# Attention of batches 2 to 7 with its large transposes on VectorE instead of TensorE

## The chip, the cores and the metric

One core of a Trainium2 chip runs the kernel. It has a TensorE (PE in the rows; PEld is its weight load), a VectorE (DVE), a ScalarE (ACT), a GpSimd (POOL) and a SyncE (SP), which issues most of the DMAs. The metric is device time in microseconds of one execution, as the median of several runs. About 0.2% of it (2.2 us) is what a measurement of this kernel can tell from no change.

## The reference

```python
# x: 8 batches x 8 heads x 512 tokens x 64;  state: 8 x 8 x 32 slots x 64
scores  = x @ state.T / 8;   a  = softmax(scores)  over the 32 slots;    xread = a  @ state
scores2 = state @ x.T / 8;   a2 = softmax(scores2) over the 512 tokens;  sread = a2 @ x
y = concat(xread, sread)     # per batch 512 + 32 rows; 4352 rows in all, 8 heads x 64 = 512 columns
h = relu(y @ w1_in) ** 2;    y = h @ w1_out          # 512 -> 2048 -> 512
h = y @ w2_in;  h = layernorm(h * softmax(h)) * g;   out = h @ w2_out    # 512 -> 1024 -> 512
```

Everything is float32. The kernel keeps that precision by splitting each operand into a high and a low float32r part and multiplying three times (high by high, high by low, low by high).

## The kernel before, in words

**The first MoE.** Its rows are worked off in nine blocks: eight batches of 512 token rows and, last, the slot rows of all batches. A block goes through 16 steps, one for each 128 of the 2048 hidden columns. In a step `hidden` multiplies the attention weights `ah`, `al` (two tiles, 128 partitions x 2 x 512) by `sw`, which is state times w1_in for that batch, so that xread is never formed: six matmuls of 512 columns into `ps_h`. ScalarE and VectorE form `r` (relu, then its square), `high` casts it to `gh`, `low` subtracts to `gl`, and `project` multiplies `gh`, `gl` by w1_out into four accumulators `acc`: 12 matmuls. A step's `project` follows the `hidden` of the step two later, so that the chain r, gh, gl has time. A step is thus 18 matmuls, and everything else on TensorE is put between them.

**sw.** The product state times w1_in lies in DRAM (`sw_d`). For four steps at a time, `load_sw` fetches it to a staging tile `stg` in DMAs on SP, and `split_sw` makes the two `sw` tiles from it: a copy on ScalarE (L119) and a subtraction on VectorE (L120). `hidden` waits for both.

**Attention of one batch** is spread over the steps of the batch before it. x of the batch comes by four DMAs in `xs`, tokens on partitions (L441). `trans_x` turns a pair of heads by four 128x128 TensorE transposes into a PSUM bank `ps_x` (L135), and `split` makes `xh`, `xl`. `scores_t` multiplies by the state, laid out block diagonally (two matmuls, L482 and L483); ScalarE copies one half of the result (L487) and VectorE adds the other (L488), so that a tile `st` holds the scores of four heads x 32 slots on partitions and 512 tokens on columns. From it two softmaxes are made.
- Over slots: `rows_a` transposes `st` to tokens on partitions (by_token, `ps_r`, L494), reduces, subtracts and takes Exp (`e`); `rows_b` sums and scales; `trans_a` transposes `e` back (`ps_a`, L135) and splits it into `ah`, `al`.
- Over tokens: `cols_a` and `cols_b` work on `st` in place (Exp with an accumulated sum, L529, then a scaling, L536); `cols_t` transposes to tokens on partitions (`ps_c`), and `sread` multiplies by x in `xs`.

**What sets the order.** Batches 0 and 1 are written out by hand. From batch 2 on, the source gives the work step by step, and a scheduler orders each engine's instructions by its own estimates when the kernel is built; on the chip each engine then runs its list in that order and waits where an operand isn't ready. `xs` has one buffer, so x of the next batch is loaded after `sread` of this one.

Of the kernel before, what the change touches and what calls it, by code (L numbers as in the profile page):

```python
# [8 lines left out]
F32 = mybir.dt.float32  # L9
F32R = mybir.dt.float32r  # L10
# [10 lines left out]
def memory_attention_relu2_solu(  # L21
# [15 lines left out]
    nc = tc.nc  # L37
    P = 128
    B, H, S, D = x.shape
# [4 lines left out]
    SO = S + NS  # L44
    NT = S // P
    NHP = H // 2
# [44 lines left out]
    xsp = pool("xsp", 1, sa, side="right")  # L91
    xtp = pool("xtp", 1, sa, side="right")
    atp = pool("atp", 2, sa, side="right")
# [3 lines left out]
    ps_a = pool("ps_a", 1, sb, space=PSUM)  # L97
# [20 lines left out]
    def split(hi, lo, src):  # L118
        nc.scalar.activation(out=hi, in_=src, func=AF.Copy)  # L119
        nc.vector.tensor_tensor(out=lo, in0=src, in1=hi.bitcast(F32), op=ALU.subtract)  # L120

    def split_bank(hi, lo, ps):

        nc.scalar.activation(out=hi, in_=ps, func=AF.Copy)

        def rest():
            nc.tensor.matmul(out=ps, lhsT=negi, rhs=hi, start=False, stop=True, skip_group_check=True)
            nc.scalar.activation(out=lo, in_=ps, func=AF.Copy)

        return rest  # L130
# [17 lines left out]
    def bank(name):  # L148
        return ps_m.tile([P, 512], F32, tag="m", name=name)
# [284 lines left out]
    xs_t = {}  # L434
    a1_t = {}

    def load_x(b):
        pl, tag = (wp, "w") if b == 1 else (xsp, "xs")
        xs_t[b] = pl.tile([P, NT, H, D], F32, tag=tag, name="xs")
        for t in range(NT):  # L440
            nc.sync.dma_start(out=xs_t[b][:, t], in_=x[b].rearrange("h (p t) d -> t p h d", t=NT)[t])  # L441

    def attention(b):

        v = {}

        def new_a1():
            a1_t[b] = tuple(a1p.tile([P, NQ, S], F32R, tag=t, name=t) for t in ("ah", "al"))

        def trans_x(hp):  # L450
            ps = ps_a.tile([P, 512], F32, tag=f"acc{hp}", name="ps_x") if b < 2 else bank("ps_x")
            transposes(ps, [xs_t[b][:, t, 2 * hp : 2 * hp + 2].rearrange("p h d -> p (h d)") for t in range(NT)])
            if b == 0:
                xh = gp.tile([P, S], F32R, tag="gh", name="xh")
                xl = gp.tile([P, S], F32R, tag="gl", name="xl")
            elif b == 1:

                if hp == 0:
                    new_a1()
                xh, xl = (a1_t[b][k][:, hp % 2, :] for k in range(2))  # L460
            else:
                xh = xtp.tile([P, S], F32R, tag="xh", name="xh")
                xl = xtp.tile([P, S], F32R, tag="xl", name="xl")
            v["rest", "x", hp] = (split_bank if b < 2 else split)(xh, xl, ps)
            v["xt", hp] = (xh, xl)

        def scores_t(hp):
# [22 lines left out]
        def by_token(tp, ps):  # L490
            for t in range(2):
                for q in range(NQ):
                    o = (t * NQ + q) * P
                    nc.tensor.transpose(  # L494
                        ps[:, o : o + P], v["st", q][:, (2 * tp + t) * P : (2 * tp + t + 1) * P], ident
                    )

        def rows_a(tp):

            ps = bank("ps_r")  # L500
            by_token(tp, ps)
            mx = smp.tile([P, 2 * H], F32, tag="mx", name="mx")
            s3 = ps.rearrange("p (g n) -> p g n", n=NS)
            nc.vector.tensor_reduce(out=mx, in_=s3, axis=AX.X, op=ALU.max)
            e = atp.tile([P, 512], F32, tag="e", name="e1")
            e3 = e.rearrange("p (g n) -> p g n", n=NS)
            nc.vector.tensor_tensor(
                out=e3, in0=s3, in1=mx.unsqueeze(2).to_broadcast([P, 2 * H, NS]), op=ALU.subtract
            )
            nc.scalar.activation(out=e, in_=e, func=AF.Exp, scale=scale)  # L510
            v["e1", tp] = e
# [55 lines left out]
        def trans_a(q):  # L567
            if q == 0 and b != 1:
                new_a1()
            ps = bank("ps_a1")  # L570
            e = [v["e1", tp].rearrange("p (t k) -> p t k", t=2) for tp in range(NT // 2)]
            transposes(ps, [e[t // 2][:, t % 2, q * P : (q + 1) * P] for t in range(NT)])
            v["rest", "a", q] = (split_bank if b < 2 else split)(a1_t[b][0][:, q, :], a1_t[b][1][:, q, :], ps)

        def rest(*k):
            v.pop(("rest", *k))()
# [29 lines left out]
    acc = {}  # L606
# [163 lines left out]
    def trans(ln):  # L770
# [7 lines left out]
            split(lh[:, a * 512 : (a + 1) * 512], ll[:, a * 512 : (a + 1) * 512], ps)  # L778
        return lh, ll

    def down(blk, t, lh, ll, final):

        ps = pools["o"].tile([P, DM], F32, tag="o", name="ps_o")
        for k in range(NK):
            wt = w2[NM + k // 2]
            o = (k % 2) * 512
            a, bb = lh[:, k * P : (k + 1) * P], ll[:, k * P : (k + 1) * P]
            nc.tensor.matmul(out=ps, lhsT=a, rhs=wt[:, 0, o : o + 512], start=(k == 0), stop=False)  # L788
            nc.tensor.matmul(out=ps, lhsT=a, rhs=wt[:, 1, o : o + 512], start=False, stop=False)  # L789
            nc.tensor.matmul(out=ps, lhsT=bb, rhs=wt[:, 0, o : o + 512], start=False, stop=(k == NK - 1))  # L790
            yield k + 1
        ob = gp.tile([P, DM], F32, tag="gh", name="ob")
        if final:

            to = out[blk * SO : blk * SO + S].rearrange("(p t) e -> p t e", t=NT)[:, t, :]
            nc.scalar.activation(out=ob[:, : DM // 2], in_=ps[:, : DM // 2], func=AF.Copy)
            nc.vector.tensor_copy(out=ob[:, DM // 2 :], in_=ps[:, DM // 2 :])
            nc.scalar.dma_start(out=to[:, : DM // 2], in_=ob[:, : DM // 2])
            nc.sync.dma_start(out=to[:, DM // 2 :], in_=ob[:, DM // 2 :])
            return  # L800
        nc.scalar.activation(out=ob, in_=ps, func=AF.Copy)
        if blk < B:
            nc.sync.dma_start(out=out[blk * SO : blk * SO + S].rearrange("(p t) e -> p t e", t=NT)[:, t, :], in_=ob)
        else:
            per = P // NS
            for bb in range(per):
                b = t * per + bb
                nc.sync.dma_start(out=out[b * SO + S : (b + 1) * SO], in_=ob[bb * NS : (bb + 1) * NS, :])
# [26 lines left out]


    att = [attention(0), attention(1)]
    steps = {}
    hid, sq, ready, left = {}, {}, {}, {}
# [66 lines left out]
    for s, (b, f) in enumerate(items):  # L906
        if s < 4 * FPC:
            continue
        w, ws = divmod(s, NF)
# [35 lines left out]
        h = high(*squares.pop(0)) if squares else None  # L945
# [4 lines left out]
        if att:  # L950
            for part in att.pop(0):
                part()
        if ws == 0 and 1 <= w < B - 1:
            load_x(w + 1)
        n = S if b < B else NSR
        if h:
# [11 lines left out]
        for e in ends.get(b, ())[1:]:  # L968
            i = f - e + 3
# [31 lines left out]
    order = [blk for blk, t in tiles if t == 0]  # L1001
# [13 lines left out]
    for s in range(1, len(tiles) + 2):  # L1015
        if s == 1:
            reload_w2(7, 1)
        if s < len(tiles):
            blk, t = tiles[s]
            i = order.index(blk) + 1  # L1020
# [7 lines left out]
            ps = up(s, blk, t)  # L1028
# [42 lines left out]
```

## Time and profile before

| | us |
|---|---|
| median of 3 runs (lowest, highest) | 1117.78 (1117.42, 1118.1) |
| span of the profiled execution | 1115.4 |
| TensorE busy | 1096.8 (98%) |
| VectorE busy | 708.5 (64%) |
| ScalarE busy | 512.4 (46%) |

The profiled execution's span is 1115.4 us; the median device time stands 2.4 us above it, which is what lies outside the span. TensorE is busy for nearly all of it; the others are averages over stages that differ much.

### The profile page before, as it was taken

The numbers are of one execution on the slowest core, as the hardware profiler recorded it, in microseconds if no ns is written. First come the engines' busy times: TensorE is split into PE (matmuls) and PEld (weight loads), VectorE is DVE, ScalarE is ACT, GpSimd is POOL, SyncE is SP. The second block draws the span as 40 slices with busy tenths as digits, with TensorE's granted clock in tenths as the row PEclk, the third lists the DMA queues.
The fourth block names the chain that finished last, engine by engine and source line by source line (L and its number), as shares of the span: only waits on it lengthen the run. The fifth ranks groups of instructions, "written<-read, shape, count | busy, mean of one in ns | idle before, by whom it ended". The sixth has DMA issues, their size and how long they took to land.

```text
span 1115.4 us, 15150 instructions
## 1 busy us (share of the span) xinstructions
PE 1096.8 (98%) x5692; PEld 911.2 (82%) x5692; DVE 708.5 (64%) x1358; ACT 512.4 (46%) x903; POOL 44.7 (4%) x62
## 2 busy tenths in 40 slices
PE   5899999999999999999999999999999999999998
PEld 4788888888888888888888889888888888888887
DVE  7999995687686695884755446664545545455443
ACT  6899776455454452442333113343433334234232
POOL 1000000010000000000000000000000000000000
PEclk9899999999999999999999999999999999999999
DMA  9779883767766632412112027410101101000001
GB/s 275 253 229 311 273 276 85 239 199 221 215 198 181 200 130 69 149 62 79 40 38 76 25 91 263 151 57 20 67 19 58 67 20 41 26 20 29 20 19 38
DMA packets 93017, 134.69 MB, mean 121 GB/s; under 512 B 44816, under 2 KB 45584, under 8 KB 92944
## 3 DMA queue, kind: packets, MB, share of 16 engines
q1 hardware_dynamic: 92224, 133.46, 37.2%
q8 instruction: 45, 0.74, 0.3%
q10 hardware_dynamic: 720, 0.26, 0.1%
q14 instruction: 28, 0.23, 0.1%
HBM read 83.37 MB, written 49.28 MB: 119 GB/s over the span
## 4 chain that ended last, share of the span: by engine, by line
PE 93%; DVE 4%; ACT 1%; DMA 1%; issue 0%; ACTq 0%; POOL 0%; DVEq 0%; POOLq 0%
PE h L738 16%; PE acc L144 11%; PE acc L145 11%; PE acc L146 11%; PE ps_h L144 6%; PE ps_h L145 6%; PE ps_h L146 6%; PE ps_o L790 6%; PE ps_o L789 6%; PE ps_o L788 6%; PE ps_t L777 3%; PE ps_sr L553 2%; PE ps_x L135 1%; PE ps_sw L388 1%; PE ps_sw L389 1%; PE ps_c L494 1%
## 5 line engine op out<-in xcount | busy, mean ns | idle before, releaser
L144 PE MATMUL acc<-gh,w1out 128*128 128x512 f32 (+1 forms) x576 | 219.0, 380 | 0.0
L146 PE MATMUL acc<-gh,w1out 128*128 128x512 f32 (+1 forms) x576 | 217.9, 378 | 0.0
L145 PE MATMUL acc<-gl,w1out 128*128 128x512 f32 (+1 forms) x576 | 217.8, 378 | 0.0
L738 PE MATMUL h<-w,x2h 128*128 128x512 f32 x544 | 148.6, 395 | 0.0
L618 ACT ACTIVATE r<-ps_h 128x512 f32<-128x512 f32 (+1 forms) x144 | 82.4, 572 | 141.1 <-PE ps_h L146 139.6
L620 DVE TENSOR_TENSOR r<-r,ps_h 128x512 f32<-128x512 f32 (+1 forms) x112 | 72.4, 647 | 89.7 <-ACT r L618 89.1
L146 PEld LDWEIGHTS acc<-gh,w1out 128*128 128x128 f32 x576 | 108.4, 188 | 20.6
L144 PEld LDWEIGHTS acc<-gh,w1out 128*128 128x128 f32 x576 | 108.4, 188 | 20.4 <-DVE ev_x L657 0.2
L145 PEld LDWEIGHTS acc<-gl,w1out 128*128 128x128 f32 x576 | 108.4, 188 | 19.9
L738 PEld LDWEIGHTS h<-w,x2h 128*128 128x128 f32 x544 | 99.6, 188 | 18.9
L144 PE MATMUL ps_h<-ah,sw 128*128 128x512 f32 x256 | 107.1, 418 | 0.0
L788 PE MATMUL ps_o<-w,lh 128*128 128x512 f32 x272 | 106.0, 390 | 0.0
L790 PE MATMUL ps_o<-w,ll 128*128 128x512 f32 x272 | 105.9, 390 | 0.0
L789 PE MATMUL ps_o<-w,lh 128*128 128x512 f32 x272 | 105.8, 389 | 0.0
L634 DVE TENSOR_TENSOR gl<-r,gh 128x512 fp32r<-128x512 f32 (+1 forms) x144 | 96.4, 669 | 11.7 <-ACT r L627 8.7
L756 ACT ACTIVATE e<-h,nm 128x1024 f32<-128x1024 f32 x34 | 38.0, 1117 | 138.8 <-DVE nm L753 138.8
L146 PE MATMUL ps_h<-ah,sw 128*128 128x512 f32 x256 | 100.9, 394 | 0.0
L145 PE MATMUL ps_h<-al,sw 128*128 128x512 f32 x256 | 100.6, 393 | 0.0
L752 DVE TENSOR_REDUCE nm<-h 128x1 f32<-128x1024 f32 x34 | 41.6, 1224 | 82.6 <-PE h L738 82.6
L738 PE MATMUL h<-w,x2l 128*128 128x512 f32 x272 | 83.8, 389 | 0.0
L764 ACT ACTIVATE j<-e,mu 128x1024 f32<-128x1024 f32 x34 | 39.1, 1151 | 54.3 <-DVE mu L761 50.3
L738 PEld LDWEIGHTS h<-w,x2l 128*128 128x128 f32 x272 | 51.1, 188 | 10.8
(173 smaller groups left out, 1723.4 us busy)
## 6 DMA issues: line engine op xcount, KB each, us to landing
stg<-sw_d SPq DMA_DIRECT2D x120, 128.0 KB, 3.1
sw_d<-ev_sw SPq DMA_DIRECT2D x28, 512.0 KB, 4.0
st<-in_moe_w_out_dram SPq DMA_DIRECT2D x24, 512.0 KB, 4.8
xs<-in_x_dram SPq DMA_DIRECT2D x32, 256.0 KB, 4.2
w1i_d<-w1in SPq DMA_DIRECT2D x16, 512.0 KB, 4.7
st<-in_moe_w_in_dram SPq DMA_DIRECT2D x16, 512.0 KB, 5.3
w1in<-w1i_d SPq DMA_DIRECT2D x32, 256.0 KB, 4.6
x_d<-ev_x SPq DMA_DIRECT2D x16, 512.0 KB, 2.7
```

The costliest lines, as they stand in the source:

```text
L144: nc.tensor.matmul(out=ps, lhsT=lh, rhs=rh, start=first and i == 0, stop=False)
L145: nc.tensor.matmul(out=ps, lhsT=lh, rhs=rl, start=False, stop=False)
L146: nc.tensor.matmul(out=ps, lhsT=ll, rhs=rh, start=False, stop=last and i == n - 1)
L618: nc.scalar.activation(out=r, in_=ps, func=AF.Relu)
L620: nc.vector.tensor_tensor(out=r, in0=r, in1=ps, op=ALU.mult)
L634: nc.vector.tensor_tensor(out=gl, in0=r, in1=gh.bitcast(F32), op=ALU.subtract)
L738: nc.tensor.matmul(out=ps[:, a * 512 : (a + 1) * 512], lhsT=lt[:, k, t * P : (t + 1) * P], rhs=w2[k][:, i, a * 512 : (a + 1) * 512], start ...
L752: nc.vector.tensor_reduce(out=nm, in_=ps, axis=AX.X, op=ALU.max)
L764: nc.scalar.activation(out=j, in_=e, func=AF.Square, bias=mu, accum_out=var)
L788: nc.tensor.matmul(out=ps, lhsT=a, rhs=wt[:, 0, o : o + 512], start=(k == 0), stop=False)
L789: nc.tensor.matmul(out=ps, lhsT=a, rhs=wt[:, 1, o : o + 512], start=False, stop=False)
L790: nc.tensor.matmul(out=ps, lhsT=bb, rhs=wt[:, 0, o : o + 512], start=False, stop=(k == NK - 1))
```

## The change

For batches 2 to 7, three transposes of each batch go from TensorE to VectorE's `transpose`, which turns every 32x32 block of a 128x512 tile on its own (L466 of the changed kernel, shown as STREAM_TRANSPOSE). Since 32x32 blocks are turned, and not 128x128, the layouts around change. x is loaded a second time, in blocks, by `load_xq`: 16 DMAs of 64 KB, each with 32 partitions x 16 x 32 floats, so that its runs in DRAM are 128 bytes long. A turn of a quarter of that tile gives `xt`, the same layout of x that TensorE's transposes gave. `rows_a` turns `st` into `e`, and `trans_a` turns `e` into `at`. There are 4 + 2 + 2 = 8 turns in a batch, in place of 16 + 8 + 8 = 32 TensorE transposes. `cols_t` and `sread` stay as they were. `xs` and the block tile `xq` take turns in the same one buffer: `load_xq` is issued in the first step of a batch, and `load_x` has moved from there to the ninth. x and the output rows of these batches are taken in plain token order, t p, not p t.

What is read by the split, the reductions and the subtraction then lies in SBUF, not in PSUM. The diff:

```diff
--- before.py
+++ after.py
@@ -437,8 +437,23 @@
     def load_x(b):
         pl, tag = (wp, "w") if b == 1 else (xsp, "xs")
         xs_t[b] = pl.tile([P, NT, H, D], F32, tag=tag, name="xs")
+        order = "h (p t) d -> t p h d" if b < 2 else "h (t p) d -> t p h d"
         for t in range(NT):
-            nc.sync.dma_start(out=xs_t[b][:, t], in_=x[b].rearrange("h (p t) d -> t p h d", t=NT)[t])
+            nc.sync.dma_start(out=xs_t[b][:, t], in_=x[b].rearrange(order, t=NT)[t])
+
+    xq_t = {}
+
+    def load_xq(b):
+
+        xq_t[b] = xsp.tile([P, NHP, S // 32, 32], F32, tag="xs", name="xq")
+        for hp in range(NHP):
+            for i in range(2):
+                for k in range(2):
+                    o = (2 * i + k) * 32
+                    nc.sync.dma_start(
+                        out=xq_t[b][o : o + 32, hp],
+                        in_=x[b, 2 * hp + i, :, k * 32 : (k + 1) * 32].rearrange("(c r) d -> r c d", r=32),
+                    )
 
     def attention(b):
 
@@ -447,21 +462,29 @@
         def new_a1():
             a1_t[b] = tuple(a1p.tile([P, NQ, S], F32R, tag=t, name=t) for t in ("ah", "al"))
 
+        def turn(out, in_):
+            nc.vector.transpose(out=out, in_=in_)
+
         def trans_x(hp):
-            ps = ps_a.tile([P, 512], F32, tag=f"acc{hp}", name="ps_x") if b < 2 else bank("ps_x")
+            if b >= 2:
+                xt = atp.tile([P, S], F32, tag="st", name="xt", bufs=4)
+                turn(xt, xq_t[b][:, hp].rearrange("p c d -> p (c d)"))
+                xh = xtp.tile([P, S], F32R, tag="xh", name="xh")
+                xl = xtp.tile([P, S], F32R, tag="xl", name="xl")
+                split(xh, xl, xt)
+                v["xt", hp] = (xh, xl)
+                return
+            ps = ps_a.tile([P, 512], F32, tag=f"acc{hp}", name="ps_x")
             transposes(ps, [xs_t[b][:, t, 2 * hp : 2 * hp + 2].rearrange("p h d -> p (h d)") for t in range(NT)])
             if b == 0:
                 xh = gp.tile([P, S], F32R, tag="gh", name="xh")
                 xl = gp.tile([P, S], F32R, tag="gl", name="xl")
-            elif b == 1:
+            else:
 
                 if hp == 0:
                     new_a1()
                 xh, xl = (a1_t[b][k][:, hp % 2, :] for k in range(2))
-            else:
-                xh = xtp.tile([P, S], F32R, tag="xh", name="xh")
-                xl = xtp.tile([P, S], F32R, tag="xl", name="xl")
-            v["rest", "x", hp] = (split_bank if b < 2 else split)(xh, xl, ps)
+            v["rest", "x", hp] = split_bank(xh, xl, ps)
             v["xt", hp] = (xh, xl)
 
         def scores_t(hp):
@@ -497,12 +520,16 @@
 
         def rows_a(tp):
 
-            ps = bank("ps_r")
-            by_token(tp, ps)
+            if b < 2:
+                ps = bank("ps_r")
+                by_token(tp, ps)
+            else:
+                ps = atp.tile([P, 512], F32, tag="e", name="e1")
+                turn(ps, v["st", tp])
             mx = smp.tile([P, 2 * H], F32, tag="mx", name="mx")
             s3 = ps.rearrange("p (g n) -> p g n", n=NS)
             nc.vector.tensor_reduce(out=mx, in_=s3, axis=AX.X, op=ALU.max)
-            e = atp.tile([P, 512], F32, tag="e", name="e1")
+            e = atp.tile([P, 512], F32, tag="e", name="e1") if b < 2 else ps
             e3 = e.rearrange("p (g n) -> p g n", n=NS)
             nc.vector.tensor_tensor(
                 out=e3, in0=s3, in1=mx.unsqueeze(2).to_broadcast([P, 2 * H, NS]), op=ALU.subtract
@@ -567,10 +594,15 @@
         def trans_a(q):
             if q == 0 and b != 1:
                 new_a1()
+            if b >= 2:
+                at = atp.tile([P, S], F32, tag="st", name="at", bufs=4)
+                turn(at, v["e1", q])
+                split(a1_t[b][0][:, q, :], a1_t[b][1][:, q, :], at)
+                return
             ps = bank("ps_a1")
             e = [v["e1", tp].rearrange("p (t k) -> p t k", t=2) for tp in range(NT // 2)]
             transposes(ps, [e[t // 2][:, t % 2, q * P : (q + 1) * P] for t in range(NT)])
-            v["rest", "a", q] = (split_bank if b < 2 else split)(a1_t[b][0][:, q, :], a1_t[b][1][:, q, :], ps)
+            v["rest", "a", q] = split_bank(a1_t[b][0][:, q, :], a1_t[b][1][:, q, :], ps)
 
         def rest(*k):
             v.pop(("rest", *k))()
@@ -778,6 +810,10 @@
             split(lh[:, a * 512 : (a + 1) * 512], ll[:, a * 512 : (a + 1) * 512], ps)
         return lh, ll
 
+    def tokens(blk, t):
+        o = out[blk * SO : blk * SO + S]
+        return o.rearrange("(p t) e -> p t e", t=NT)[:, t, :] if blk < 2 else o[t * P : (t + 1) * P, :]
+
     def down(blk, t, lh, ll, final):
 
         ps = pools["o"].tile([P, DM], F32, tag="o", name="ps_o")
@@ -792,7 +828,7 @@
         ob = gp.tile([P, DM], F32, tag="gh", name="ob")
         if final:
 
-            to = out[blk * SO : blk * SO + S].rearrange("(p t) e -> p t e", t=NT)[:, t, :]
+            to = tokens(blk, t)
             nc.scalar.activation(out=ob[:, : DM // 2], in_=ps[:, : DM // 2], func=AF.Copy)
             nc.vector.tensor_copy(out=ob[:, DM // 2 :], in_=ps[:, DM // 2 :])
             nc.scalar.dma_start(out=to[:, : DM // 2], in_=ob[:, : DM // 2])
@@ -800,7 +836,7 @@
             return
         nc.scalar.activation(out=ob, in_=ps, func=AF.Copy)
         if blk < B:
-            nc.sync.dma_start(out=out[blk * SO : blk * SO + S].rearrange("(p t) e -> p t e", t=NT)[:, t, :], in_=ob)
+            nc.sync.dma_start(out=tokens(blk, t), in_=ob)
         else:
             per = P // NS
             for bb in range(per):
@@ -951,6 +987,8 @@
             for part in att.pop(0):
                 part()
         if ws == 0 and 1 <= w < B - 1:
+            load_xq(w + 1)
+        if ws == 8 and 1 <= w < B - 1:
             load_x(w + 1)
         n = S if b < B else NSR
         if h:
```

Three places in the order of the two kernels follow; names are as above, a number behind `acc` or `e` tells buffers apart, and the brackets hold what an instruction waits for.

First TensorE at batch 5's attention. Before, around the second score product of batch 5 (`ps_s`, L482 and L483):

```order
L146 MATMUL acc_4060<-gh,w1out 128x512
L482 MATMUL ps_s<-xh,bd_2_159 128x512 [waits DVE_49,Activation_49]
L483 MATMUL ps_s<-xl,bd_2_159 128x512 [waits DVE_49]
L135 MATMUL ps_x<-ident,xs 128x128 [waits PE_49]
L135 MATMUL ps_x<-ident,xs 128x128 x3
L144 MATMUL ps_h<-ah,sw 128x512
L145 MATMUL ps_h<-al,sw 128x512
```

and after, at the third and the fourth score product (L505 and L506):

```order
L146 MATMUL acc_4042<-gh,w1out 128x512
L505 MATMUL ps_s<-xh,bd_2_156 128x512 [waits PE_49,Activation_49]
L506 MATMUL ps_s<-xl,bd_2_156 128x512 [waits DVE_49]
L505 MATMUL ps_s<-xh,bd_2_159 128x512 [waits PE_49,Activation_49]
L506 MATMUL ps_s<-xl,bd_2_159 128x512 [waits DVE_49]
L517 MATMUL ps_c<-ident,st 128x128 [waits PE_49]
L517 MATMUL ps_c<-ident,st 128x128 [waits DVE_49]
L144 MATMUL ps_h<-ah,sw 128x512 [waits Activation_49]
L145 MATMUL ps_h<-al,sw 128x512
```

Before, a `hidden` (`ps_h`) of six matmuls stands behind each score product, and a `project` of 12 behind that; after, the third and the fourth product stand side by side, with nothing of the first MoE between them or before the next `hidden`.

Then ScalarE at the same place: `sw<-stg` is the split of sw for the next four `hidden`. Before:

```order
L119 ACTIVATE xh<-ps_x 128x512 [waits PE_49]
L487 ACTIVATE st<-ps_s 64x512 [waits PE_49]
L119 ACTIVATE xh<-ps_x 128x512 [waits DVE_49,PE_49]
L119 ACTIVATE sw<-stg 128x512 [waits DMAHW7_49,PE_49]
L618 ACTIVATE r<-ps_h 128x512 [waits PE_49]
L119 ACTIVATE sw<-stg 128x512
L487 ACTIVATE st<-ps_s 64x512 [waits PE_49]
```

and after, from the copy of the third score product on:

```order
L510 ACTIVATE st<-ps_s 64x512 [waits PE_49]
L119 ACTIVATE xh<-xt 128x512 [waits DVE_49,Activation_49]
L119 ACTIVATE ah<-at 128x512 [waits DVE_49]
L510 ACTIVATE st<-ps_s 64x512 [waits PE_49]
L556 ACTIVATE st,cs<-st,cm 128x512 [waits DVE_49]
L119 ACTIVATE sw<-stg 128x512 [waits DMAHW3_49,DMAHW4_49,DMAHW2_49,DMAHW1_49]
L119 ACTIVATE sw<-stg 128x512
```

Before, the split stands behind the first score copy; after, it stands behind the fourth score copy and the Exp of the second softmax (L556, `cols_a`).

Last, ScalarE at batch 2's attention. Before:

```order
L325 ACTIVATE ev_sw<-ps_sw 128x512 [waits PE_49]
L119 ACTIVATE sw<-stg 128x512 [waits DMAHW6_49,DMAHW5_49]
L487 ACTIVATE st<-ps_s 64x512 [waits PE_49]
L225 ACTIVATE w1in<-ch 128x512 [waits DVE_49]
L119 ACTIVATE xh<-ps_x 128x512 [waits PE_49]
L119 ACTIVATE sw<-stg 128x512 [waits DMAHW7_49,DMAHW0_49]
```

and after, from the copy of the second score product on:

```order
L510 ACTIVATE st<-ps_s 64x512 [waits PE_49]
L119 ACTIVATE xh<-xt 128x512 [waits DVE_49,Activation_49]
L556 ACTIVATE st,cs<-st,cm 128x512 [waits DVE_49]
L537 ACTIVATE e_1954<-e_1954 128x512 [waits DVE_49]
L563 ACTIVATE st<-st,cs 128x512 [waits DVE_49,Activation_49]
L119 ACTIVATE sw<-stg 128x512 [waits DMAHW2_49,DMAHW1_49]
L119 ACTIVATE sw<-stg 128x512 [waits DMAHW4_49,DMAHW3_49]
```

Before, the two splits stand around the first score copy; after, they stand behind both Exps of the first half (L556, L537) and the scaling (L563).

## Rows read from the trace of the kernel before

**Rows 1.** The page: busy time (x instructions), then 40 slices of the span in tenths.

```profile
PE 1096.8 (98%) x5692; PEld 911.2 (82%) x5692; DVE 708.5 (64%) x1358; ACT 512.4 (46%) x903; POOL 44.7 (4%) x62
...
PE   5899999999999999999999999999999999999998
...
PEclk9899999999999999999999999999999999999999
```

**Rows 2.** The page: the chain that ended last, share of the span by engine.

```profile
PE 93%; DVE 4%; ACT 1%; DMA 1%; issue 0%; ACTq 0%; POOL 0%; DVEq 0%; POOLq 0%
```

**Rows 3.** Busy us of each engine in stretches (from:to), PEclk, DMA share, GB/s.

```profile
150.00:160.00 10.00, 10.00 (x48) 8.27 (x47) 9.85 (x20) 7.30 (x14) 0.00 (x0) 1.00 0.62 203
160.00:170.00 10.00, 10.00 (x50) 8.27 (x49) 9.97 (x20) 8.26 (x16) 0.00 (x0) 1.00 0.93 288
280.00:360.00 80.00, 80.00 (x425) 65.70 (x424) 54.45 (x103) 40.37 (x71) 5.51 (x4) 1.00 0.65 195
360.00:440.00 80.00, 80.00 (x452) 65.50 (x451) 58.97 (x111) 32.90 (x59) 5.29 (x4) 1.00 0.46 139
```

**Rows 4.** PE's groups, 90 to 700 us: line, operation, xcount, busy us, mean ns.

```profile
L135 PE MATMUL ps_x<-ident,xs 128*128 128x128 f32 x96 | 15.0, 272 | 0.0
...
L135 PE MATMUL ps_a<-ident,e 128*128 128x128 f32 x48 | 7.4, 272 | 0.0
L494 PE MATMUL ps_r<-ident,st 128*128 128x128 f32 x48 | 7.2, 272 | 0.0
```

**Rows 5.** PE in order of time at 301 us: start, duration, instruction.

```profile
301.47 0.39 PE L145 MATMUL acc<-gl,w1out 128*128 128x512 f32 x1
301.70 0.40 PE L146 MATMUL acc<-gh,w1out 128*128 128x512 f32 x1
301.93 0.60 PE L135 MATMUL ps_x<-ident,xs 128*128 128x128 f32 x4
302.29 0.49 PE L144 MATMUL ps_h<-ah,sw 128*128 128x512 f32 x1
302.61 0.39 PE L145 MATMUL ps_h<-al,sw 128*128 128x512 f32 x1
```

**Rows 6.** DVE's groups, 90 to 700 us: xcount, busy us, mean ns, idle before.

```profile
L488 DVE TENSOR_TENSOR st<-ps_s,st 64x512 f32<-64x512 f32 x24 | 16.5, 687 | 15.6 <-ACT st L487 15.4
...
L526 DVE TENSOR_REDUCE cm<-st 128x1 f32<-128x512 f32 x12 | 8.2, 680 | 0.2
...
L228 DVE TENSOR_SCALAR cz<-ch 128x512 uint32<-128x512 uint32 x17 | 7.2, 422 | 0.2
...
L120 DVE TENSOR_TENSOR w<-st,w 128x1024 fp32r<-128x1024 f32 x5 | 6.1, 1223 | 2.5 <-ACT w L119 1.7 <-DMA w1in<-w1i_d 0.8
```

**Rows 7.** ACT's groups, 90 to 700 us, the same columns.

```profile
L119 ACT ACTIVATE sw<-stg 128x512 fp32r<-128x512 f32 x57 | 35.5, 626 | 36.5 <-PE ps_h L146 31.8 <-DMA stg<-sw_d 4.1
...
L487 ACT ACTIVATE st<-ps_s 64x512 f32<-64x512 f32 x24 | 14.2, 593 | 36.7 <-PE ps_s L483 36.7
...
L529 ACT ACTIVATE st<-st,cm 128x512 f32<-128x512 f32 x12 | 8.6, 717 | 3.8 <-PE ps_r L494 3.8
...
L510 ACT ACTIVATE e<-e 128x512 f32<-128x512 f32 x12 | 7.5, 626 | 2.8 <-DVE e L507 2.8
...
L529 ACT ACTIVATION_READ_ACCUMULATOR st<-st,cm 128x1 f32 x12 | 2.3, 188 | 0.0
```

**Rows 8.** ACT at batch 5's first two scores: start, duration, instruction.

```profile
383.27 0.59 ACT L487 ACTIVATE st<-ps_s 64x512 f32<-64x512 f32 x1 [2.16 <-PE ps_s L483]
...
384.41 0.64 ACT L119 ACTIVATE sw<-stg 128x512 fp32r<-128x512 f32 x1
...
388.29 0.59 ACT L487 ACTIVATE st<-ps_s 64x512 f32<-64x512 f32 x1 [2.07 <-PE ps_s L483]
```

**Rows 9.** DMA from 205.6 to 211.4 us, x loads: packets, MB, share of 16 engines.

```profile
DMA packets 4261, 1.23 MB, mean 212 GB/s; under 512 B 4173, under 2 KB 4173, under 8 KB 4261
...
q1 hardware_dynamic: 4261, 1.23, 89.1%
```

## The prediction

> **What bounds the kernel now.** The page first: TensorE is busy for 1096.8 of 1115.4 us, full in every slice but the first few and the last, and its clock is granted at nearly ten tenths, the 2.4 GHz level [rows 1]. The chain that ended last runs over TensorE for 93% [rows 2]. Then the stretches in which attention of batches 2 to 7 lies: TensorE is busy for all 80 of 80 us [rows 3], so it waits for nothing there, and each operation taken off it is a gain, as long as the others still deliver in time. They differ. VectorE is busy 54 to 59 of 80 us at batches 4 and 5, but 9.85 and 9.97 of 10 us between 150 and 170 us, where batch 2's attention lies beside the last conversions of w_out [rows 3]. So the question is not what VectorE adds on average, but where its added work, or the new order, makes TensorE wait.
>
> **What goes from TensorE.** 96 + 48 + 48 = 192 transposes of 128x128 [rows 4]. Their durations of 272 ns overlap and aren't their cost; the pitch is. Four begin at 301.93, the second matmul after them at 302.61: 0.68 us, of which one matmul takes its usual 0.23 (301.70 less 301.47) [rows 5]. That leaves 0.45 us for a group of four; 48 groups make 21.6 us. With nothing late anywhere that is the whole gain.
>
> **What a turn costs VectorE.** No row of before shows one. On a 128x512 tile of 4-byte elements a copy-like operation takes 0.42 us, a reduction or a two-operand one 0.68, and twice the elements 1.22 [rows 6]. I take 0.68, the middle, since a reduction walks a tile once as a turn must, and keep 0.42 and 1.22. 48 turns are then 33 us of VectorE over six batches, 5.4 in each: 59 of 80 becomes 63, still cover, except at batch 2. The other operations stay in number, and read SBUF instead of PSUM; I put their change at nothing, within 0.05 us each by the copies on ScalarE from either (0.59 for the score copy out of PSUM, 0.63 for the split of sw out of SBUF [rows 7]).
>
> The Trainium skill speaks against the change here: "VectorE: DVE Perf Modes", in "Rules for kernel authors", gives a 128x128 transpose to TensorE if PSUM will do for its result, and in "The three transpose paths" lists 390 ns for TensorE and 311 for VectorE, in bf16. The first figure does not hold in this kernel, where the pitch is a quarter of it [rows 5]; the second would make a turn 4 x 0.311 = 1.24 us, an estimate by that page, close to my upper bound.
>
> **What the second x load costs.** Between 205.6 and 211.4 us x comes in 256-byte packets: 4261 packets use 89.1% of 16 engines for 5.8 us, 19.4 ns a packet [rows 9]. The new load has 8192 packets of 128 bytes: 9.9 us if a packet takes as long, 5.0 if it goes by bytes. I take 8. The DMA engines have room for it at batches 4 and 5 (shares 0.65 and 0.46 [rows 3]). But it stands ahead of the next `stg` loads on SP, in 16 issues, and the first x transposes now wait only for a quarter of the block load. The moved `load_x` stands in the ninth step, and `sread`, which alone still needs `xs`, in the last two: five steps of 4.1 us (18 x 0.23) cover its 5.8, so it costs nothing.
>
> **Where TensorE will wait: the new order.** The order of the changed kernel differs from before in more than the missing transposes, and two places are bad.
>
> *Batch 5, the third and fourth score product.* Before, 5.0 us lie between one score copy on ScalarE and the next (383.27 to 388.29), with the split of sw between them, at 384.41 [rows 8], and ScalarE waits 2.1 us for each product: the chain has time. After, the third and fourth stand with no matmul between, and the split of sw behind the fourth's Exp, so TensorE has nothing to do while the chain passes. I count it with the durations of [rows 6, 7] and 0.68 for a turn.
> - From the second product to the third: the third's xh stands on ScalarE behind the Exp of the first half's e. Score copy 0.59, add 0.69, turn 0.68, two reductions 1.36, subtraction 0.68, Exp 0.63, xh 0.6: 5.2, and the third x's turn in between 0.7, 5.9. The 19 matmuls that lie there cover 19 x 0.23 = 4.4. Wait: 1.5.
> - From the third to the fourth: score copy 0.59, add 0.69, the turn of the fourth x 0.68, xh 0.6, xl 0.69: 3.3 and a few signals. No cover. Wait: 3.4.
> - From the fourth to the next `hidden`: score copy 0.59, add 0.69, turn 0.68, two reductions 1.36, Exp 0.72 with its accumulator read 0.19, split of sw 0.63: 4.9, with signals 5.0; covered by nothing but transposes for the second softmax. Then its low part on VectorE: 0.7.
>
> Together 10.6 us. Bounds: 5 if only the last of them is exposed, 14 if the subtraction and later `hidden` are late as well.
>
> *Batch 2.* VectorE has 0.15 and 0.03 us left of 10 [rows 3]; six of the batch's eight turns fall there, 6 x 0.68 = 4.1. Here too the split of sw has gone behind both Exps, which adds its low part, 0.7. What VectorE does there is what TensorE needs next (gl, evacuations, sw), so I take it as exposed: 4.8. Bounds: 0 (if the lag of two steps absorbs it) and 9 (it also holds the products at 0.7 each on six further steps).
>
> *Batches 3 and 4.* At each one evacuation or load behind the 16 DMAs is late: half of the 2.5 us by which the 16 issues stay behind four (8 us less the 5.8 of [rows 9], plus signals), 1.3 each. Bounds 0 and 4. *Batches 6 and 7* keep the old lag; 0.5 for both.
>
> **Sum.** Against the profiled execution: 1115.4 - 21.6 + 10.6 + 4.8 + 2.6 + 0.5 = 1112.3 us of span. The median lies 2.4 above the span (1117.8 against 1115.4), so 1114.7.
>
> **The rivals.**
> - *The full gain.* The chains fit, since each engine has slack before it and the lag of two steps takes up what is late. For it: TensorE waits for nothing now, and ScalarE's idle time of 2 us before each score copy [rows 8] shows that the chain runs ahead. Against it: the fourth product and the next `hidden` stand with nothing to cover them. If at most 6 us of waits arise: 1117.8 - 21.6 + 3 = 1099, between 1096 and 1102.
> - *Slower by the turn's price.* If a turn takes 1.22 us, 0.54 more, it is paid wherever a turn stands in an exposed chain: five at batch 5, six at batch 2, and some eight at the other batches (two each): 19 x 0.54 = 10.3 us, so 1125. It decides from where 19 times the excess eats the 3.1 us of gain and the 2.2 that can be told: an excess of 0.28, a turn of 0.96 us. By the skill's 1.24 the sum is 1125 too, an estimate by the page named above.
> - *Slower by the block load.* If the 8192 packets and 16 issues take 15 us and not 8, `stg` behind them comes 7 us later in each batch; two steps hide part of it, and batches 3 and 4, which already wait, pay 3 to 5 each: 1114.7 + 8 = 1123. For it: runs of 128 bytes, half of anything that before moves in bulk; against it: the DMA share falls to 0.46 by batch 5. The Trainium skill, "DMA: Bandwidth & Descriptors", "Rules for kernel authors", calls transfers under 64 KB mostly overhead; these are at 64 KB, and no run here has timed one of them.
> - *That it doesn't do what it says* I leave out: the order shows 192 transposes fewer and 48 turns.
>
> **How the numbers follow.** Forecast 0.55, full gain 0.17, dear turn 0.14, slow load 0.14. Within the forecast the waits add up to 10 to 25 us, so 1106 to 1121; of its 0.55 I put 0.32 below 1115.5 (faster by over 0.2%), 0.20 within 2.2 us of 1117.8, 0.03 above 1120. Faster: 0.32 + 0.17 = 0.49, rounded to 0.50. Same: 0.20, and 0.02 of the slow load. Slower: 0.03 + 0.14 + 0.11, 0.28. The range for eight times in ten reaches into both sides: 1101 to 1125. The likeliest case's own is 1106 to 1121.
>
> **What would show it.** The group of the turns gives 0.68 us or not. TensorE's waits, none now, should show two heaps: about 10 us around batch 5's scores, most of it ended by ScalarE's split of sw and by xh, and about 5 at batch 2, ended by VectorE; little at batches 6 and 7. The block load should land in 8 us. I am wrong if TensorE's waits between 90 and 620 us are under 6 us, or over 25, or if most of them lie at batches that I left out.

## The result: 1126.7 us, slower by 0.8%

| | before | after |
|---|---|---|
| median, us | 1117.94 | 1126.72 |
| span of the profiled execution, us | 1115.4 | 1125.7 |

The ratio is 1.0082, with a 95% interval from 1.0067 to 1.0096. That is clear of no change, on the other side of the forecast, and just outside the range (1101 to 1125).

The page of the changed kernel, busy time and slices, answers to [rows 1], and its chain to [rows 2]:

```profile
PE 1088.6 (97%) x5500; PEld 894.6 (79%) x5500; DVE 731.9 (65%) x1406; ACT 509.0 (45%) x903; POOL 45.6 (4%) x62
...
PE   5899989999999979999999999999999999999998
...
PEclk9899989999989989999999999999999999999999
```

```profile
PE 89%; DVE 6%; DMA 2%; ACT 2%; issue 1%; SPq 1%; POOL 0%; DVEq 0%; ACTq 0%; POOLq 0%
```

TensorE is busy for 8 us less, not 21.6, the span is 10.3 longer, and there is a slice at seven tenths, and several of a lower clock, where before all were full. The stretches of [rows 3], again:

```profile
150.00:160.00 10.00, 9.11 (x38) 6.52 (x36) 7.03 (x17) 7.83 (x16) 0.00 (x0) 1.00 0.53 183
160.00:170.00 10.00, 6.49 (x14) 4.27 (x15) 9.84 (x19) 6.08 (x12) 0.00 (x0) 0.66 0.69 207
280.00:360.00 80.00, 75.95 (x369) 59.82 (x368) 55.40 (x103) 35.12 (x65) 3.24 (x2) 0.96 0.67 188
360.00:440.00 80.00, 71.86 (x359) 56.59 (x358) 55.08 (x102) 32.22 (x59) 4.21 (x3) 0.94 0.51 139
```

TensorE was busy throughout in all four; now it is for 6.49 of 10 us at batch 2 and 71.86 of 80 at batch 5, and the granted clock is under 1.00 in three of the four. What TensorE waited for between 90 and 640 us (us in total, times, longest); before, there was no wait of it in the stretches of [rows 3]:

```profile
PE ps_s L505 <- ACT xh L119: 6.4, 3, 2.7
PE ps_h L144 <- ACT sw L119: 5.8, 2, 3.0
PE ps_h L146 <- DVE sw L120: 1.8, 4, 0.7
PE ps_c L517 <- DVE st L511: 1.2, 1, 1.2
PE ps_s L505 <- ACT ev_sw L325: 1.1, 1, 1.1
```

With smaller ones these are 17.1 us. The turns on VectorE (x count, busy us, mean ns) answer to the bounds of [rows 6]:

```profile
L466 DVE STREAM_TRANSPOSE xt<-xq 128x512 f32<-128x512 f32 x24 | 16.9, 702 | 0.1
...
L466 DVE STREAM_TRANSPOSE e<-st 128x512 f32<-128x512 f32 x12 | 8.5, 704 | 0.1
L466 DVE STREAM_TRANSPOSE at<-e 128x512 f32<-128x512 f32 x12 | 8.4, 698 | 0.0
```

A turn takes 0.70 us, as forecast (0.68).

**Where the time is.** From the start of the 17th `hidden` to that of the 125th, start times of matmuls give a full account. The stretch takes 517.4 us before and 527.1 after, 9.7 more. The transposes are 21.6 less. What came instead, counted as each start's distance from the one before beyond the usual 0.23 (0.11 for a transpose): 22.8 us more in distances over 0.45 us (the waits with the slow matmul behind each), 6.0 in distances of 0.43, and 2.6 in smaller ones: -21.6 + 22.8 + 6.0 + 2.6 = 9.8. Another 0.9 lies ahead of that stretch.

By place, the 23.1 us of long distances are 6.3 at batch 2, 1.0 at batch 3, 4.9 at batch 4, 10.6 at batch 5, 0.2 behind. Batch 5 on TensorE, from the third score product on (start, duration, instruction, idle time before it and what ended it):

```profile
402.30 0.50 PE L505 MATMUL ps_s<-xh,bd 128*128 128x512 f32 x1 [1.07 <-ACT xh L119]
403.03 0.50 PE L506 MATMUL ps_s<-xl,bd 128*128 128x512 f32 x1 [0.23 <-DVE xl L120]
406.27 0.79 PE L505 MATMUL ps_s<-xh,bd 128*128 128x512 f32 x1 [2.74 <-ACT xh L119]
407.00 0.79 PE L506 MATMUL ps_s<-xl,bd 128*128 128x512 f32 x1
407.59 0.41 PE L517 MATMUL ps_c<-ident,st 128*128 128x128 f32 x1
409.20 0.47 PE L517 MATMUL ps_c<-ident,st 128*128 128x128 f32 x1 [1.19 <-DVE st L511]
412.53 0.80 PE L144 MATMUL ps_h<-ah,sw 128*128 128x512 f32 x1 [2.86 <-ACT sw L119]
413.12 0.63 PE L145 MATMUL ps_h<-al,sw 128*128 128x512 f32 x1
413.55 0.63 PE L144 MATMUL ps_h<-ah,sw 128*128 128x512 f32 x1
```

and on ScalarE:

```profile
407.83 0.59 ACT L510 ACTIVATE st<-ps_s 64x512 f32<-64x512 f32 x1 [1.07 <-PE ps_s L506]
411.14 0.72 ACT L556 ACTIVATE st<-st,cm 128x512 f32<-128x512 f32 x1 [2.73 <-DVE cm L554]
411.77 0.19 ACT L556 ACTIVATION_READ_ACCUMULATOR st<-st,cm 128x1 f32 x1
411.86 1.13 ACT L119 ACTIVATE sw<-stg 128x512 fp32r<-128x512 f32 x2
```

The reader sees the chain of the prediction link by link. The third product waits 1.1 us (forecast 1.5) and the fourth 2.7 (3.4). From there to the next `hidden` TensorE waits 1.2 us ahead of a transpose of `st` and 2.9 ahead of the `hidden` itself (5.0), and not at all for the low part (0.7). The `hidden` waits for the split of sw, which stands on ScalarE behind the Exp (411.14) that needs the fourth product. And the last three matmuls of the first fence show what the prediction did not have: after the waits one starts 0.59 and 0.43 us behind the other, not 0.23.

### The profile page after: what moved, and what is told of

The parts are those of the page before. It is cut to its first block, busy times and chain, and to the rows that moved or that the text cites. A ratio compares the mean times of both kernels' runs of the same rounds, so it can differ in the third digit from the quotient of the medians.

```text
span 1125.7 us, 14936 instructions
## 1 busy us (share of the span) xinstructions
PE 1088.6 (97%) x5500; PEld 894.6 (79%) x5500; DVE 731.9 (65%) x1406; ACT 509.0 (45%) x903; POOL 45.6 (4%) x62
## 4 chain that ended last, share of the span: by engine, by line
PE 89%; DVE 6%; DMA 2%; ACT 2%; issue 1%; SPq 1%; POOL 0%; DVEq 0%; ACTq 0%; POOLq 0%
PE h L770 16%; PE acc L144 10%; PE acc L145 10%; PE acc L146 10%; PE ps_h L144 6%; PE ps_h L146 6%; PE ps_o L826 5%; PE ps_o L824 5%; PE ps_o L825 5%; PE ps_h L145 5%; PE ps_t L809 3%; PE ps_sr L580 2%; DMA st64w<-in_moe_w_in_dram 1%; DMA stg<-sw_d 1%; PE ps_sw L388 1%
## 5 line engine op out<-in xcount | busy, mean ns | idle before, releaser
L144 PEld LDWEIGHTS acc<-gh,w1out 128*128 128x128 f32 x576 | 109.7, 190 | 21.1 <-DVE ev_x L689 0.9
L146 PEld LDWEIGHTS acc<-gh,w1out 128*128 128x128 f32 x576 | 109.4, 190 | 20.4
L144 PE MATMUL ps_h<-ah,sw 128*128 128x512 f32 x256 | 103.5, 404 | 5.8 <-ACT sw L119 5.8
L146 PE MATMUL ps_h<-ah,sw 128*128 128x512 f32 x256 | 100.8, 395 | 1.8 <-DVE sw L120 1.8
L666 DVE TENSOR_TENSOR gl<-r,gh 128x512 fp32r<-128x512 f32 (+1 forms) x144 | 94.3, 656 | 11.1 <-ACT r L659 8.9
L144 PEld LDWEIGHTS ps_h<-ah,sw 128*128 128x128 f32 x256 | 48.7, 190 | 17.2 <-ACT sw L119 7.5
```

The costliest lines, as they stand in the source:

```text
L144: nc.tensor.matmul(out=ps, lhsT=lh, rhs=rh, start=first and i == 0, stop=False)
L146: nc.tensor.matmul(out=ps, lhsT=ll, rhs=rh, start=False, stop=last and i == n - 1)
L666: nc.vector.tensor_tensor(out=gl, in0=r, in1=gh.bitcast(F32), op=ALU.subtract)
```

## The experiments

Theory A: 16 block loads on SP, which are slow, make the scheduler that orders the kernel at build time expect `stg` late. It then packs products and projects together and puts the split of sw behind the attention chain; the waits and the clock behind them are the loss. Theory B: the turns make VectorE's chains too long. Theory C: the many 128-byte packets crowd the DMA engines. (What the scheduler expects is inferred from the orders that it made; its estimates stand in no run.)

The lag, in the expectations and below, is the place of a step's `project`, with its own `hidden` counted in: in the kernel before it stands behind the `hidden` of the step two later, a lag of three. The kernel before was measured again beside each set of runs: 1118.5 us beside softmax alone, x alone, the load alone and ScalarE's queue; 1119.1 beside GpSimd's queue, each turn twice and work in the waits; 1118.6 beside the other three.

**Softmax alone.** The change without its x part: x by TensorE, loaded once, softmax turned.

```diff
-                turn(xt, xq_t[b][:, hp].rearrange("p c d -> p (c d)"))
+            transposes(ps, [xs_t[b][:, t, 2 * hp : 2 * hp + 2].rearrange(...) for t in range(NT)])
-            load_xq(w + 1)
```

> Only the two softmax turns are on VectorE (4 turns a batch), x is transposed by TensorE and loaded once; 96 transposes less, 10.8 us. Theory A (the 16 block loads on SP stand ahead of the stg loads, and the scheduler then puts the split of sw behind the attention chain; the waits and the half clock behind them are the loss): that is gone, the lag of the project is three steps everywhere, so 1106 to 1110 us, no wait of TensorE between 90 and 620 us over 1 us, granted clock 1.00. Theory B (the turns themselves make VectorE's chains too long): half of the turns, half of the loss, 1118 to 1124 us.

Measured 1105.9, ratio 0.9889 (0.9872 to 0.9905): 12.6 us faster than before, for 10.8 us of transposes. TensorE's only wait in 90 to 640 us:

```profile
PE acc L144 <- ACT ev_x L686: 0.8, 1, 0.8
```

So half of the turns cost nothing that can be measured. Theory B fails here, and A holds (its range was 1106 to 1110).

**x alone.** The reverse: `load_xq` and the four turns of x stay, softmax goes back to TensorE.

```diff
-                turn(ps, v["st", tp])
+            by_token(tp, ps)
```

> Only x is turned on VectorE, with the second load in blocks; the softmax is transposed by TensorE as before. Theory A: all of the loss stays (about 30 us, waits near batches 2, 4 and 5 and the clock at half behind them), and only 10.8 us are saved: 1130 to 1140 us. Theory B: half of the turns, 1118 to 1124 us.

Measured 1133.0, ratio 1.0130 (1.0114 to 1.0145), within A's range. Most of the loss is in the x part: this kernel lies 25.3 us above 1118.5 - 10.8, the changed one 30.4 above 1117.9 - 21.6, and the softmax-only kernel has none, so that some 5 us arise only where both parts are there. In the order of this kernel, as in that of the changed one, the `project` of the 68th step stands directly behind its own `hidden`: a lag of one, not three.

**The load alone.** Before, with the block load added and read by nobody.

```diff
             load_x(w + 1)
+            load_xq(w + 1)       # its tile lies in DRAM
```

> The kernel before, with the 16 block loads of a batch added on SP behind the x load, into a scratch tensor in DRAM that nothing reads; all transposes on TensorE, no turn. Theory A: the split of sw and the lag collapse at the same steps as in the changed kernel, so waits and low clock at batches 2, 4 and 5 as there: 1130 to 1150 us. Theory B: no turn, 1116 to 1120 us. Theory C: a few us slower, without waits for the split of sw.

Measured 1145.9, ratio 1.0244 (1.0229 to 1.0259). Without one turn and with all transposes on TensorE, the added load costs 27 us. In its order the lag falls at the same steps (19, 20, 23, 67, 68) as in the changed kernel. Its largest waits on TensorE:

```profile
PE ps_a L135 <- DVE e L537: 5.6, 2, 4.9
PE ps_s L500 <- ACT xh L119: 2.8, 2, 1.7
PE ps_sw L388 <- DMA w1in<-w1i_d: 2.8, 2, 2.2
```

They lie at batches 2, 4 and 5, as A had it, but A's detail is not borne out: of 15.9 us in all, only 0.4 are ended by the split of sw. The 4.9 us at batch 5 end with the softmax chain; the split stands behind that chain here too (it starts at 421.4, its loads had landed by 404.6). And 2.8 us are ended by a load itself, of w1in: in this kernel some of the loss is loads that come late on the chip.

**The same bytes in four loads.** As the run before, but x by 4 DMAs of 256 KB with runs of 256 bytes.

```diff
-                    nc.sync.dma_start(out=xq_t[b][o : o + 32, hp], in_=x[b, 2 * hp + i, ...])    # 16 times
+            nc.sync.dma_start(out=xq_t[b][:, t]..., in_=x[b].rearrange(...)[t])                   # 4 times
```

> As the run with the added load alone (x loaded again into a scratch tensor, no turn), with the same bytes in 4 DMAs of 256 KB with runs of 256 bytes, as the x load itself, on SP at the same place. The order of the engines keeps the lag of three steps here. Theory A1 (the loss comes through the order that the scheduler makes of the 16 slow loads): 1117 to 1121 us. Theory A2 (the loss comes because SP and the DMA engines are late on the chip, whatever the order): half or more of the 27 us stay, 1130 us or more.

Measured 1117.2, ratio 0.9987 (0.9978 to 0.9997): nothing left of the 27 us. The order keeps its lag of three steps, and TensorE waits nowhere between 90 and 640 us. So it isn't the bytes. Nor is it the plain token order, which this kernel and the load alone share with the changed one.

**Sixteen small loads.** 16 DMAs again, each with a quarter of its tokens.

```diff
-                        out=xq_t[b][o : o + 32, hp],
+                        out=xq_t[b][o : o + 32, hp, :4],
```

> The added load alone, 16 DMAs on SP as in the changed kernel, each with a quarter of its bytes (512 KB less x 1.5 a batch left out); the lag of three steps is kept. Theory A1: 1117 to 1120 us. If it is the number of issues on SP: 1125 us or more.

(What is left out is three quarters of the 1 MB of each batch.) Measured 1118.2, ratio 0.9997 (0.9987 to 1.0006). Nor is it the number of issues by itself. With the loads small the order is good, and so is the time.

**The loads on ScalarE's queue.** The changed kernel with one word changed.

```diff
-                    nc.sync.dma_start(
+                    nc.scalar.dma_start(
```

> The changed kernel with the 16 block loads of a batch issued on ScalarE's queue, not SP's; all 48 turns and all bytes stay. Theory A: the split of sw is back before the chain, lag three steps, so 1117.9 - 21.6 and up to 6 us of waits: 1096 to 1103 us. Theory B and theory C (the 128-byte packets crowd the DMA engines): as the changed kernel, 1124 to 1129 us, since the turns and the packets are the same.

Measured 1139.2, ratio 1.0189 (1.0173 to 1.0205): A's forecast missed by 36 us. The order was good. But each issue waits until an earlier load has landed, and ScalarE, which works, stood behind. Even at batch 6, where those landings lay back, the 16 issues held it for 8.9 us (467.0 to 475.9). Its largest wait, and TensorE's:

```profile
ACT r L650 <- DMA xq<-in_x_dram: 73.4, 6, 18.9
```

```profile
PE ps_h L144 <- DVE r L652: 31.0, 5, 11.3
```

Six batches, 12 us each, and the `r` of a `hidden` behind it. The run does not tell A from B by its time; it puts a new wait in the place of the old one, which I had not asked about.

**The loads on GpSimd's queue.** The same word, `nc.gpsimd`.

> The changed kernel with the 16 block loads of a batch on GpSimd's queue, which is nearly idle; all 48 turns and all packets stay. Theory A (the order that the SP loads bring about, and what follows from it): the lag is three steps again and no busy engine is held up by the issues, as ScalarE was with 73 us in its run: 1096 to 1106 us. Theory B or C (the turns, or the packets): as the changed kernel, 1124 to 1129.

Measured 1102.2, ratio 0.9853 (0.9838 to 0.9867): 16.9 us faster than before and 24.5 faster than the changed kernel, with the same turns and the same bytes to load. TensorE's waits:

```profile
PE acc L145 <- DVE gl L666: 1.5, 2, 1.2
PE ps_sw L144 <- DVE st L511: 0.7, 1, 0.7
PE acc L144 <- DVE ev_x L689: 0.6, 1, 0.6
PE ps_s L505 <- ACT xh L119: 0.6, 2, 0.4
```

This is the fastest version here, and B falls with it. It still lies 6 us above 1117.9 - 21.6 (4.7 above 1119.1 - 21.6, by the kernel before beside it). For C it says less than I expected: on this queue the profile counts the same bytes in 3072 packets of 2 KB (packets, MB, share of 16 engines),

```profile
q0 software_dynamic: 3072, 6.30, 2.5%
```

so the 128-byte packets are gone too. The run on ScalarE's queue does have them,

```profile
q10 hardware_dynamic: 51408, 6.56, 3.6%
```

and there TensorE's waits other than those behind ScalarE's held-up `r` are 4.0 us, none of them ended by a DMA. That speaks against C.

**Each turn twice.** The softmax-only kernel with every turn made two times.

```diff
             nc.vector.transpose(out=out, in_=in_)
+            nc.vector.transpose(out=out, in_=in_)
```

> The kernel with only the softmax turned, each turn made twice: 24 turns more, 24 x 0.70 = 16.9 us more of VectorE. Theory A: with the lag at three steps VectorE has room, 1105 to 1109 us. Theory B: the turns' length is what makes the chains late, 1112 to 1125 us.

Measured 1106.2, ratio 0.9889 (0.9873 to 0.9906), against 1105.9 with one turn: 17 us more of VectorE cost 0.3 us or nothing. With a good order a turn of the softmax could be twice as dear.

**Work in the waits.** The changed kernel with matmuls that keep TensorE busy where it waited.

```diff
+            if b in (2, 5) and hp >= 2:
+                for _ in range(10):
+                    nc.tensor.matmul(out=ps, lhsT=lt, rhs=a1_t[b - 1][0][:, 0, :], start=True, stop=True)
```

> The changed kernel with 10 matmuls more, whose result is overwritten, ahead of each of the third and fourth score products of batches 2 and 5: 40 x 0.23 = 9.1 us of work put where TensorE waits. They cover about 7.5 us of waits. If the low clock behind the waits costs as the granted clock says (some 7 us at these two batches), it stays at 1.00 there and the time is 1119 to 1123 us, under the changed kernel's 1126.7 in spite of the added work. If the clock isn't what costs, 1127 to 1130 us.

Measured 1127.6, the changed kernel 1126.7. That lies in the range given for "the clock isn't what costs": the expected gain did not come, though 9.1 us of added work cost only 0.9. The two stretches behind batch 2's and batch 5's waits (busy us, PEclk):

```profile
163.80:169.80 6.00, 5.79 (x24) 4.29 (x23) 5.97 (x11) 2.61 (x5) 0.00 (x0) 1.00 0.72 192
412.00:416.50 4.50, 4.44 (x11) 3.49 (x12) 3.01 (x6) 2.26 (x5) 0.00 (x0) 0.51 0.50 154
```

At batch 2 the clock now stays at 1.00, where it was 0.50 in the changed kernel; but from the 21st to the 25th `hidden` it takes 1.5 us more than before, against 1.8 in the changed kernel: 4.6 us of work went where waits and half clock had been. At batch 5 the wait for the split of sw remained and the clock fell behind it. In the account's stretch, starts 0.43 apart cost 3.2 us, not 6.2, long distances 15.7, not 23.1, smaller ones 1.2 more: 9.1 - 3.0 - 7.4 + 1.2 = -0.1, and the stretch is as long as in the changed kernel (527.1). So the account closes, but the run does not show what the changed kernel would take at full clock: at batch 2 the end may as well be set by VectorE, busy 19.4 of the 20 us from 160 to 180. That the slow starts behind batch 2's wait could be won back is thus not shown.

**The load alone on GpSimd.** One word of the load-alone kernel.

```diff
-                    nc.sync.dma_start(        # in the load-alone kernel
+                    nc.gpsimd.dma_start(
```

> The added load alone, all of its 16 DMAs and bytes, on GpSimd's queue; no turn; lag of three steps. Theory A1: 1117 to 1122 us, and what it lies above 1118 is the load's share of the 6 us by which the changed kernel with its loads on GpSimd stays behind a saving of 21.6. If the packets themselves crowd the DMA engines (theory C): 1130 us or more.

Measured 1128.4, ratio 1.0083 (1.0067 to 1.0099). This run is not the test it was meant to be. The loads, whose target nothing reads, had nothing to wait for (first and last start behind the durations):

```profile
L453 POOL DMA_DIRECT2D xq<-in_x_dram x96: 650/650/886, 4.6 to 84.2; - x96
```

All 96 were issued in the first 84 us, beside the loads of the weights, so its 10 us are the price of that collision and not of the loads in their place: its 17th `hidden` starts at 136.2 us, 11.1 later than in the kernel before, and from there to the 125th it takes 518.2 us (517.4). The share of the loads in the 6 us that the GpSimd version lies above the full gain stays open. Of those, by the same account, 2.5 lie ahead of the 17th `hidden` and 3.5 between it and the 125th; in each of the two, one turn of x waits for the block load (1.1 and 1.0 us).

## Why the prediction was wrong

*The gain on TensorE, 21.6 us:* right. It stands in the account, and the softmax-only kernel got its half.

*The turn, 0.68 us:* right, 0.70, and the rival of a dear turn is out. The 1.24 us worked out from the Trainium skill ("VectorE: DVE Perf Modes", "The three transpose paths") is not what this tile takes, and the page's rule to leave such transposes to TensorE ("Rules for kernel authors") did not pay in this kernel, where TensorE is full: the softmax-only kernel is 12.6 us faster.

*Batch 5, 10.6 us of waits:* right in place and chain; in size partly by luck. TensorE's idle time there is 8.1 us (3.8 for xh, 2.9 for the split of sw, 1.2 for `st`, 0.2 for xl). The long distances come to the forecast's 10.6 because they hold the slow matmuls behind the waits, which the forecast did not have.

*Batch 2, 4.8:* 4.3 of idle time, 6.3 of long distances. I had priced a full VectorE as one lump; the waits are 2.5 us for xh, 1.1 for a copy on ScalarE (ev_sw), 0.4 for an evacuation on VectorE and 0.3 for the low part of sw.

*Batches 3 and 4, 1.3 each:* too little at batch 4. I priced there only what the 16 issues hold up directly, and did not follow the split of sw, as I had done at the other two. It is late at batch 4 too. SP is in the block load for 8.7 us, and the four `stg` loads are issued behind it (start, duration of the issues, x count):

```profile
292.90 8.71 SPq L453 DMA_DIRECT2D xq<-in_x_dram  x15
...
302.25 2.38 SPq L403 DMA_DIRECT2D stg<-sw_d  x4
```

and on ScalarE the split then stands behind an operation that converts a weight (L186):

```profile
309.74 0.72 ACT L186 ACTIVATE ce<-ce,rebias 128x512 int32<-128x512 int32 x1 [1.13 <-DVE ce L185]
310.37 1.14 ACT L119 ACTIVATE sw<-stg 128x512 fp32r<-128x512 f32 x2
```

TensorE's `hidden` waits from 308.1 to 311.0, and twice more for the low part: 4.1 us of idle time, 4.9 of long distances, not 1.3. At batch 3 the long distances are 1.0. And the block load goes at the pace of its issues, 0.58 us each here (8.71 for 15), so that from the first issue to the last landing it takes 10.1 to 12.7 us at batches 3 to 7, not 8.

*The sum: this step failed; a term was missing.* It took waits as lost time alone, and put what comes behind a wait at nothing. The idle time was nearly right, 17.1 us against 18.5 (batch 4's shortfall and batch 5's surplus about cancel), so the sign set for being wrong, waits under 6 or over 25 us, did not show. But 32.3 us were lost. Behind a wait the clock falls. Batch 2:

```profile
160.55 0.50 PE L505 MATMUL ps_s<-xh,bd 128*128 128x512 f32 x1 [1.11 <-ACT ev_sw L325]
...
163.84 0.79 PE L505 MATMUL ps_s<-xh,bd 128*128 128x512 f32 x1 [2.54 <-ACT xh L119]
...
165.77 0.80 PE L144 MATMUL acc<-gh,w1out 128*128 128x512 f32 x1 [0.41 <-DVE ev_x L689]
...
166.78 0.63 PE L146 MATMUL acc<-gh,w1out 128*128 128x512 f32 x1
167.21 0.63 PE L144 MATMUL acc<-gh,w1out 128*128 128x512 f32 x1
...
170.26 0.40 PE L146 MATMUL acc<-gh,w1out 128*128 128x512 f32 x1
```

After 1.1 and 2.5 us of idle time starts are 0.43 apart for 3 us, and only then 0.23 again. The three stretches in which this is so (busy us of TensorE first, PEclk behind the POOL column):

```profile
163.80:169.80 6.00, 5.55 (x12) 3.77 (x13) 5.91 (x11) 2.33 (x4) 0.00 (x0) 0.50 0.74 216
312.60:319.90 7.30, 6.58 (x16) 4.82 (x16) 3.54 (x5) 0.60 (x1) 0.59 (x1) 0.54 0.57 183
403.00:415.40 12.40, 5.58 (x12) 3.37 (x13) 10.59 (x22) 5.33 (x10) 0.00 (x0) 0.59 0.56 137
```

Busy time times what the clock lacks is 5.55 x 0.50 + 6.58 x 0.46 + 5.58 x 0.41 = 8.1 us; 6.0 of them are starts 0.43 apart, the rest is inside the long distances. In the stretch that the prediction rests on, the clock was at 1.00 throughout [rows 3], since there was no wait; the sum used that pitch for a kernel that waits. Its 18.5 us of waits against 22.8 + 6.0 + 2.6 + 0.9 = 32.3 us found, with the long distances in place of the waits: 6.0 are starts at the lower clock, 3.6 batch 4, 1.5 batch 2, 2.6 the small restarts, and 0.9 the stretch ahead of batch 2, which the prediction took as unchanged; batches 3, 6 and 7 came some 0.6 cheaper. This is an account of where the time lies. That a kernel at full clock would be shorter by it is not shown: with work in the waits the clock stayed up at batch 2, and the time did not fall.

*The rivals.* A dear turn and the full gain are out. The slow block load comes nearest in time (1123) and in place (batch 4), and part of its condition was met: the load took up to 12.7 us, where I had 8 and the rival 15. But it priced batches 3 and 4 alone, at 8 us more than my sum, and they gave 5.9 of long distances against 2.6. Its reason, small packets, is not borne out either: they took no more than I had put in (with ScalarE's queue 3.6% of 16 engines, 1136.7 us and 51408 packets make 12.7 ns each, 6.5 us for 8192), the same bytes in four loads cost nothing, and on GpSimd's queue the whole change is 1.5% faster than before.

*Order or late loads.* No kernel here has the 16 slow loads on SP and the good order at once. But the changed kernel's trace tells the two apart for its waits. The `stg` of batch 5's split is loaded here (start, duration of the issues, x count; then KB each and the median time from issue to landing):

```profile
388.20 2.50 SPq L410 DMA_DIRECT2D stg<-sw_d  x4
...
stg<-sw_d SPq DMA_DIRECT2D x4, 128.0 KB, 3.3
```

The last of the four landed at 393.6, and ScalarE came to the split at 411.86, 18.2 us later: the split is late by its place in the order, not by its load. At batch 4 the last landed at 308.6 and the split began at 310.37, directly behind the weight conversion, which waited for VectorE. No wait of TensorE between 90 and 640 us is ended by a load, and no turn of x waits for the block load; ScalarE and VectorE wait 4.4 us for loads between 120 and 640 us, less than the 17.2 of the kernel before. So the changed kernel's waits, as far as its trace tells, come from the order; how the loads on SP lead the scheduler to that order is inferred. In the load alone, where 2.8 us are ended by a load, the shares stay open.

## What to carry to other kernels

When a scheduler orders the engines, read a change first as a change of its input: one slow item on a shared queue can move work that the diff doesn't touch, and a load alone, with nothing that reads it, shows that. Where TensorE is full, a wait can cost more than its idle time (here 32.3 us lost for 17.1 of idle time), so price what follows it as well; and follow the late split to every batch, not only to the worst. A queue is chosen by what else its engine does: the same loads cost 24 us more on SP than on GpSimd's queue, and 37 more on ScalarE's, where each issue held up its arithmetic.

## What the runs showed that was not expected

- TensorE's clock fell to its lower level, 1.2 GHz (granted 0.50 to 0.59 over the stretches shown, starts 0.43 us apart), behind the waits of batches 2, 4 and 5, and TensorE worked on at that level before it rose; beside the 3.4 us of waits in the GpSimd version it stayed at 1.00.
- 32x32 turns of a 128x512 float32 tile take 0.70 us on VectorE, and 24 of them more cost 0.3 us in all in the softmax-only kernel.
- A DMA of 64 KB with runs of 128 bytes is issued on SP in 0.49 us (median), and 16 in a row go at the pace of the issues.
- On ScalarE's queue 16 such loads held the engine for 12 us a batch on average.
- The same 16 loads a batch, read by nobody, made the kernel before 27 us longer on SP: its other work was ordered anew around them.
